# Softmax denominators: from a ones product, Ln and Exp to a transposed sum, a reciprocal and a transpose on VectorE

## The chip, the cores and the metric

The kernel runs on one core of a Trainium2 chip. The metric is the device time of a whole execution in microseconds; the number given for a kernel is the median of several executions. Beside it stands one execution taken by the hardware profiler, with every instruction of the engines TensorE (PE), VectorE (DVE), ScalarE (ACT), GpSimd (POOL) and SyncE (SP), the last of which only issues transfers here.

## The reference

Attention over 32 learned memory slots a head, followed by a gated feed-forward block. There are 8 batches of 8 heads, 576 tokens, head size 64; the feed-forward block goes from 512 to 1536 and back.

```python
a = exp(phi - max(phi, axis=2));  a = a / (sum(a, axis=2) + 1e-09)
k_m = einsum('bhsm,bhsd->bhmd', a, k);  v_m = einsum('bhsm,bhsd->bhmd', a, v)
scores = q @ k_m.T / sqrt(64)                      # per head: 576 tokens x 32 slots
attn = exp(scores - max(scores));  attn = attn / (sum(attn, axis=-1) + 1e-09)
x = attn @ v_m                                     # heads side by side: 4608 x 512
out = (silu(x @ w_gate) * (x @ w_val)) @ w_out     # 4608 x 512, float32
```

The change concerns the last division of attention: the sum over the 32 slots, for every token and head.

## The kernel before, in words

**Layout.** The scores of a batch lie with slots along the partitions: a tile `es[b, g]` of 128 partitions (four heads of 32 slots) by 2 halves of 288 tokens, for each of two groups `g` of heads. Summing over slots thus means summing over blocks of 32 partitions. `z_inv` does it with TensorE: a product with `bones`, a 128x128 matrix with four 32x32 blocks of ones on its diagonal, gives every partition the sum of its own head. ScalarE then takes Ln of it from PSUM (L427) and Exp of the negative (L429), which is the reciprocal in `lz`; both functions and the Exp of the scores are in one table. `norm` (L434) multiplies on VectorE and leaves the weights `t_A`.

**The value projection is folded.** `v_m` is multiplied into the gate and value weights first (`u_round`, tiles `t_U`), so that `gv_half` (L497) computes gate and value for 128 of 1536 features and 288 tokens by two products over `t_A`, one for each group. `gv_gate` puts a Silu on the gate (ScalarE, L513), the pending `mul` multiplies it with the value (VectorE, L520) into `t_h`. A batch has 24 such slots. `out_units` (L557) are the products of `t_h` with `w_out`: 12 for each tile of 128 tokens, then a copy of the tile from PSUM to `t_o` by VectorE (L569) or ScalarE (L567), and transfers to DRAM on SP's queue. A batch's list of out products (`out_list`) has 4 or 5 tiles, and is worked off in the batch after it: it is the filler that `take(n)` hands out wherever TensorE would wait.

**Order.** All instructions are issued in an order written out by hand (`manual_schedule`); each engine works through its own in that order. Batches 0 and 1 are done together at the start, with a code of their own. For batches 2 to 7 the loop at the end does: four out products; `u_values`, the fourth of the six parts of `t_U` (8 products, two copies at L478); `scores` for both groups, each with two Exp (L413); Exp of phi for the next batch; `z_inv` for both groups; a switch to the table with Silu (L804); `norm` for both groups. In between stand out products, 32 from the scores to the first slot. Then the 24 slots with the rest of the out products spread among them, and in their midst the key and value sums of the next batch (`kv_items`: L233 and L265 to L295), the last two parts of this batch's `t_U` (`u_item`) and the first three of the next (`u_three`). At the end of a batch comes the switch back to the table with Exp and Ln (L655).

**Other queues.** Keys, values, q and phi of later batches are loaded on POOL's queue; q is transposed by a transfer on SP's queue (`load_qT`, L120). From batch 4 on POOL also adds up Exp of phi for the next batch (`phi_sum`); it begins with a copy, `t_mark` (L213), that waits for `t_A` of group 1. PSUM has eight banks, taken from one list in turn (`bank`, `done`); `t_o` has three buffers.

Of the kernel before, what the change touches and what calls it, by code (L numbers as in the profile page):

```python
# [9 lines left out]
FP32 = mybir.dt.float32  # L10
# [4 lines left out]
def kernel(  # L15
# [19 lines left out]
    nc = tc.nc  # L35
# [8 lines left out]
    NG = 2  # L44
    NP = H // 2
    NJF = DF // 128
    HALF = S // 2
    CH = 512
    NCH = DF // CH
    sm_scale = 1.0 / math.sqrt(D)  # L50
# [347 lines left out]
    def scores(b, g):  # L398
        p = gv_banks()
        for i in range(NP):  # L400
            for r in range(2):
                nc.tensor.matmul(  # L402
                    p[r][32 * i:32 * i + 32, 0:HALF],
                    lhsT=kTs[b][64 * r:64 * r + 64, g, 32 * i:32 * i + 32],
                    rhs=qTs[b, i][64 * r:64 * r + 64, g],
                    start=True,
                    stop=True,
                    tile_position=(64 * r, 32 * i),
                )
        e = att.tile([128, 2, HALF], BF16, tag=f"E{g}", name="t_E")  # L410
        for r in range(2):
            scale = rks[b][:, g:g + 1] if b in rks else sm_scale
            nc.scalar.activation(out=e[:, r], in_=p[r][:, 0:HALF], func=AF.Exp, scale=scale)  # L413
        done(*p)
        es[b, g] = e
# [3 lines left out]
    def z_inv(b, g):  # L419

        p = gv_banks()
        lz = att.tile([128, 2, HALF], FP32, tag="lz", bufs=3, name="t_lz")
        for r in range(2):
            nc.tensor.matmul(  # L424
                p[r][:, 0:HALF], lhsT=bones, rhs=es[b, g][:, r], start=True, stop=True
            )
            nc.scalar.activation(out=lz[:, r], in_=p[r][:, 0:HALF], func=AF.Ln)  # L427
        done(*p)
        nc.scalar.activation(out=lz, in_=lz, func=AF.Exp, scale=-1.0)  # L429
        lzs[b, g] = lz  # L430

    def norm(b, g):
        a = att.tile([128, 2, HALF], BF16, tag=f"A{g}", name="t_A")
        nc.vector.tensor_tensor(out=a, in0=es.pop((b, g)), in1=lzs.pop((b, g)), op=ALU.mult)  # L434
        atts[b, g] = a
# [6 lines left out]
    def u_round(b, parts, evac):  # L442


        banks = []
        for which, c, halves in parts:
            w0, w1, h0, h1 = which[0], which[-1] + 1, halves[0], halves[-1] + 1
            n = (h1 - h0) * HC
            p = [bank([128, CH], FP32, f"p_u{g}") for g in range(NG)]
            for w in which:  # L450
                o = (w - w0) * n
                for i in range(NP):
                    for g in range(NG):
                        nc.tensor.matmul(  # L454
                            p[g][32 * i:32 * i + 32, o:o + n],
                            lhsT=kTs[b][64 * g:64 * g + 64, 2, 32 * i:32 * i + 32],
                            rhs=w_part(w, c, i, g, halves),
                            start=True,
                            stop=True,
                            tile_position=(64 * g, 32 * i),  # L460
                        )
            for g in range(NG):
                if (b, c, g) not in Us:
                    Us[b, c, g] = upool.tile([128, 2, 2, HC], BF16, tag=f"U{c}{g}", name="t_U")
                if len(which) == 1:
                    dst = Us[b, c, g][:, h0:h1, w0]
                else:
                    dst = Us[b, c, g][:, h0]
                src = p[g][:, 0:(w1 - w0) * n].rearrange("p (a f) -> p a f", f=HC)
                banks.append((dst, src, p[g], rSs[b][:, g:g + 1] if b in scaled else None))  # L470
        for (t, p, home, r), e in zip(banks, evac):
            if e == "a":
                if r is None:
                    nc.scalar.copy(out=t, in_=p)  # L474
                else:
                    nc.scalar.activation(out=t, in_=p, func=AF.Copy, scale=r)  # L476
            elif r is None:
                nc.vector.tensor_copy(out=t, in_=p)  # L478
            else:
                nc.vector.tensor_scalar(out=t, in0=p, scalar1=r, scalar2=None, op0=ALU.mult)  # L480
            done(home)
# [67 lines left out]
    def out_units(c, u, eng):  # L549

        mine = {}

        def unit(jf):
            def run():
                if jf == 0:
                    mine["p"] = bank([128, DM], FP32, "p_oo")
                nc.tensor.matmul(  # L557
                    mine["p"],
                    lhsT=hts[c, jf][:, 128 * u:128 * (u + 1)],
                    rhs=WO[jf],  # L560
                    start=(jf == 0),
                    stop=(jf == NJF - 1),
                )
                if jf == NJF - 1:
                    t_o = work.tile([128, DM], FP32, tag="to", name="t_o")
                    if eng == "a":
                        nc.scalar.copy(out=t_o, in_=mine["p"])  # L567
                    else:
                        nc.vector.tensor_copy(out=t_o, in_=mine["p"])  # L569
                    done(mine["p"])  # L570
                    for (r0, m, bb, jj, pp) in token_segments(2 * c * S + 128 * u, 128):
                        nc.sync.dma_start(
                            out=out_r[bb, jj, pp:pp + m, :], in_=t_o[r0:r0 + m, :]
                        )

            return run

        return [unit(jf) for jf in range(NJF)]
# [32 lines left out]
    def out_list(b):  # L611
        tiles = range(0, 4) if b % 2 == 0 else range(4, 9)
        res = []
        for n, u in enumerate(tiles):
            if b + 1 == B and u == tiles[-1]:
                res += out_units_end(b // 2, u)
            else:
                res += out_units(b // 2, u, "v" if n % 4 != 3 else "a")
        return res

    def q_items(b, evac):
# [15 lines left out]

    def u_values(b):

        u_round(b, (((1,), 1, (0, 1)),), "vv")  # L640
    def run(items):
        for x in items:
            x()
# [131 lines left out]
    def take(n):  # L775
        nonlocal backlog
        n = max(0, min(n, len(backlog)))
        part, backlog = backlog[:n], backlog[n:]
        return part

    for b in range(2, B):
        last = b + 1 == B
        exp_tables()
        if b == 2:
            load_qT(2)
            phi_exp(2)
            run(take(28))
            run(kv_items(2)[:1] + take(6) + kv_items(2)[1:] + take(14))
        run(take(4))
        u_values(b)  # L790
        for g in range(NG):
            scores(b, g)
        if b == 2:
            load_k(3)
            load_v(3)
            load_q(4)
            load_phi(4, nc.gpsimd)
        run(take(6))
        if not last:
            phi_exp(b + 1)  # L800
        z_inv(b, 0)
        run(take(1))
        z_inv(b, 1)
        nc.scalar.preload_act_table_set("silu_and_others")  # L804
        run(take(13))
        norm(b, 0)
        norm(b, 1)
        if b == 2:
            run(take(4))
            u_three(2)  # L810
        run(take(12))
        g = gv_slots(b)
        beside = 0 if last else 7
        outs = [lambda: run(take(1)) for _ in range(len(backlog) - beside)]
        streams = [(g, 0, 24), (outs, 0, 24)]
        if last:
            streams += [([u_item(b, 2)], 5, 6)]
        if b == 2:
            streams += [
                ([lambda: load_qT(3)], 12, 12),  # L820
                (kv_items(3, lambda: (u_item(2, 2)(), run(take(2)))), 10, 14),
                ([lambda: (run(take(2)), u_three(3), run(take(3)))], 17, 18),
            ]
        elif not last:
            load_qT(b + 1)
        if not last:
            if b > 2:
                phi_sum(b + 1)
            if b + 3 < B:
                load_q(b + 3)  # L830
            if b + 2 < B:
                load_k(b + 2)
                load_v(b + 2)
            if b + 3 < B:
                load_phi(b + 3, nc.gpsimd)
        if not last and b > 2:
            streams += [
                (kv_items(b + 1, lambda: (u_item(b, 2)(), run(take(2)))), 9, 14),
                ([lambda: (run(take(2)), u_three(b + 1), run(take(3)))], 17, 18),
            ]  # L840
        spread(*streams)
        flush_mul()
        backlog += out_list(b)
# [29 lines left out]
```

The softmax here doesn't subtract the row's maximum and nothing guards it: scores larger than these inputs give would overflow.

## Time and profile before

| | |
|---|---|
| median of 11 executions | 246.91 us (246.66 to 247.24) |
| the profiled execution, own time | 247.4 us |
| its span, first to last instruction | 245.5 us |
| TensorE busy | 233.7 us (95%), granted clock 0.999 |
| VectorE busy | 164.0 us (67%) |
| ScalarE busy | 165.0 us (67%) |
| GpSimd busy | 47.6 us (19%) |
| transfers | 37.00 MB, mean 151 GB/s |

Busy times are of engines that work beside each other, and do not add up to the span. In a row of the groups, the line, the engine and the operation come first, then what is written and what is read with the shape and the count; then the busy time in all, the mean length of one in ns, and the time that the engine idled ahead of them with what ended it. Matmuls run one into the next, so the mean length of one is more than the time that it takes from the queue; that is read from the distance between two starts. In the timeline a row has the start, the length, the engine, the line and the count; an idle time ahead of it stands in brackets with what ended it.

### The profile page before, as it was taken

What the parts mean: (1) busy time and instruction counts of PE and PEld (TensorE: products, weight loads), DVE (VectorE), ACT (ScalarE), POOL (GpSimd) and SP (SyncE); (2) the same over time, 40 slices, a digit from 0 to 9 for tenths busy, and PEclk for the clock granted to TensorE, in tenths of its full rate; (3) what the DMA queues carried; (4) which work ended last, traced back from release to release, by engine and by line L of the source; (5) the groups of instructions that cost most, each with busy time, mean ns of one, the idle gap of its engine ahead of it and who ended that gap; (6) DMA issues with size and microseconds to landing.
All of it is one profiled execution on the core that took longest, in us unless ns stands there. A gap on an engine that the chain in (4) does not pass through costs nothing.

```text
span 245.5 us, 6474 instructions
## 1 busy us (share of the span) xinstructions
PE 233.7 (95%) x2508; PEld 141.5 (58%) x2535; DVE 164.0 (67%) x368; ACT 165.0 (67%) x350; POOL 47.6 (19%) x77
## 2 busy tenths in 40 slices
PE   7997999999999999999999999999999999999993
PEld 2553567674445656477646655476546655567542
DVE  4257699992348688479837887489846876587320
ACT  2768789893096567957895677766995668676201
POOL 8432522000050004051305130070005000000000
PEclk9999999999999999999999999999999999999999
DMA  7999999996899986993995499389326221310144
GB/s 209 204 205 205 201 207 208 255 251 91 175 152 235 236 191 81 220 310 81 156 275 152 76 166 262 112 160 168 72 47 147 38 45 43 85 45 1 45 117 97
DMA packets 42447, 37.00 MB, mean 151 GB/s; under 512 B 15920, under 2 KB 37168, under 8 KB 42416
## 3 DMA queue, kind: packets, MB, share of 16 engines
q0 software_dynamic: 21424, 22.42, 52.9%
q1 hardware_dynamic: 20240, 13.37, 22.8%
q10 hardware_dynamic: 752, 0.79, 1.0%
q8 instruction: 20, 0.33, 0.5%
q14 instruction: 11, 0.09, 0.1%
HBM read 42.47 MB, written 9.44 MB: 211 GB/s over the span
## 4 chain that ended last, share of the span: by engine, by line
PE 76%; DMA 17%; POOL 3%; issue 2%; ACT 0%; POOLq 0%
PE p_oo L557 30%; PE p_g L497 19%; PE p_v L497 18%; DMA t_kv<-in_v_dram 14%; PE p_u L454 5%; DMA t_qT<-t_q 3%; PE p_kv L233 2%; POOL t_q L107 1%; POOL t_kv L97 1%; DMA out_dram<-t_o 1%; PE p_g L424 1%; PE p_v L424 0%; PE p_g L402 0%; POOL t_q L114 0%; POOL t_kv L101 0%
## 5 line engine op out<-in xcount | busy, mean ns | idle before, releaser
L557 PE MATMUL p_oo<-WO,t_h 128*128 128x512 bf16 x393 | 101.8, 379 | 3.0 <-issue 2.9
L513 ACT ACTIVATE t_sg<-p_g 128x288 bf16<-128x288 f32 x192 | 76.4, 414 | 33.5 <-PE p_g L497 26.7
L520 DVE TENSOR_TENSOR t_h<-t_sg,p_v 128x288 bf16<-128x288 bf16 x192 | 82.4, 452 | 17.3 <-PE p_v L497 12.6
L497 PEld LDWEIGHTS <-t_U 128*128 128x128 bf16 x768 | 73.8, 98 | 31.7 <-issue 2.5
L497 PE MATMUL p_g<-t_A,t_U 128*128 128x288 bf16 x384 | 77.7, 286 | 0.4
L497 PE MATMUL p_v<-t_A,t_U 128*128 128x288 bf16 x384 | 76.9, 286 | 0.0
L557 PEld LDWEIGHTS <-t_h 128*128 128x128 bf16 x420 | 39.5, 98 | 41.0 <-issue 5.9
L569 DVE COPY t_o<-p_oo 128x512 f32<-128x512 f32 x27 | 18.7, 691 | 31.4 <-PE p_oo L557 31.3
L478 DVE CAST t_U<-p_u 128x512 bf16<-128x512 f32 x42 | 26.7, 684 | 6.8 <-PE p_u L454 6.8
L474 ACT CAST t_U<-p_u 128x512 bf16<-128x512 f32 x30 | 15.8, 592 | 8.1 <-PE p_u L454 8.1
L567 ACT COPY t_o<-p_oo 128x512 f32<-128x512 f32 x8 | 4.7, 588 | 20.5 <-PE p_oo L557 10.6
L114 POOL DMA_DIRECT2D t_q<-in_q_dram x6 | 4.8, 800 | 62.7 <-DMA t_qT<-t_q 61.2
L454 PE MATMUL p_u<-W,t_kT 64*32 64x512 bf16 (+1 forms) x416 | 16.0, 364 | 0.1
L668 PE MATMUL p_warm<-bones 128*128 128x512 bf16 (+2 forms) x43 | 12.7, 423 | 1.7 <-DVE bones L691 1.7
L434 DVE TENSOR_TENSOR t_A<-t_E,t_lz 128x576 bf16<-128x576 bf16 x16 | 11.5, 751 | 0.3 <-ACT t_lz L429 0.2
L213 POOL COPY t_mark<-t_A 1x1 bf16<-1x1 bf16 x4 | 0.7, 182 | 55.7 <-DVE t_A L434 55.7
L429 ACT ACTIVATE t_lz<-t_lz 128x576 f32<-128x576 f32 x16 | 10.9, 682 | 0.5
L655 ACT ACT_TABLE_LOAD x7 | 9.0, 1283 | 1.4 <-PEq L857 1.3
L476 ACT ACTIVATE t_U<-p_u,t_rS 128x512 bf16<-128x512 f32 (+1 forms) x14 | 8.1, 628 | 2.1 <-PE p_u L454 2.1
L454 PEld LDWEIGHTS <-t_kT 64*32 64x32 bf16 x416 | 4.9, 89 | 8.0 <-issue 6.8
L480 DVE TENSOR_SCALAR t_U<-p_u,t_rS 128x512 bf16<-128x512 f32 (+1 forms) x14 | 8.8, 669 | 1.0 <-PE p_u L454 1.0
L668 PEld LDWEIGHTS <-bones 128*128 128x128 bf16 x43 | 4.4, 109 | 7.1 <-issue 3.0
(67 smaller groups left out, 169.5 us busy)
## 6 DMA issues: line engine op xcount, KB each, us to landing
t_kv<-in_k_dram POOLq DMA_DIRECT2D x8, 576.0 KB, 9.9
t_kv<-in_v_dram POOLq DMA_DIRECT2D x8, 576.0 KB, 14.1
out_dram<-t_o SPq DMA_DIRECT2D x23, 192.0 KB, 2.5
t_phi<-in_phi_dram POOLq DMA_DIRECT2D x6, 576.0 KB, 16.6
t_q<-in_q_dram POOLq DMA_DIRECT2D x6, 576.0 KB, 8.0
out_dram<-t_o SPq DMA_DIRECT2D x24, 128.0 KB, 2.6
WO<-in_moe_w_out_dram POOLq DMA_DIRECT2D x3, 512.0 KB, 19.2
out_dram<-t_o SPq DMA_DIRECT2D x23, 64.0 KB, 2.0
```

What stands on the lines that cost most here:

```text
L429: nc.scalar.activation(out=lz, in_=lz, func=AF.Exp, scale=-1.0)
L434: nc.vector.tensor_tensor(out=a, in0=es.pop((b, g)), in1=lzs.pop((b, g)), op=ALU.mult)
L454: nc.tensor.matmul(p[g][32 * i:32 * i + 32, o:o + n], lhsT=kTs[b][64 * g:64 * g + 64, 2, 32 * i:32 * i + 32], rhs=w_part(w, c, i, g, halve ...
L474: nc.scalar.copy(out=t, in_=p)
L478: nc.vector.tensor_copy(out=t, in_=p)
L497: nc.tensor.matmul(p[:, 0:HALF], lhsT=Us[b, c, g][:, o // 2, which, 128 * (o % 2):128 * (o % 2 + 1)], rhs=atts[b, g][:, r], start=(g == 0) ...
L513: nc.scalar.activation(out=sg, in_=gate[:, 0:HALF], func=AF.Silu)
L520: nc.vector.tensor_tensor(out=dst, in0=sg, in1=val[:, 0:HALF], op=ALU.mult)
L557: nc.tensor.matmul(mine["p"], lhsT=hts[c, jf][:, 128 * u:128 * (u + 1)], rhs=WO[jf], start=(jf == 0), stop=(jf == NJF - 1),)
L569: nc.vector.tensor_copy(out=t_o, in_=mine["p"])
L655: nc.scalar.preload_act_table_set("natural_log_exp_and_others")
L668: nc.tensor.matmul(p[:, 0:128 * a], lhsT=bones, rhs=x.to_broadcast([128, a, 128]) if a > 1 else bones, start=True, stop=True,)
```

## The change

The denominators of batches 2 to 7 are no longer computed by `z_inv`. A new function, `z_inv_v`, does it on VectorE alone. A sum with `apply_transpose` turns each 32x32 block of `es` (32 slots by 32 tokens) and adds along the slots, so that the sums of a token stand on the partition of its place in its block of 32 tokens: the 2 x 288 columns are 18 blocks, and the sums are a tile of 128x18. Then comes the reciprocal, and a 32x32 transpose that reads each reciprocal 32 times over and so hands it back to all 32 slots of its head. `norm` is as before. Batches 0 and 1 keep `z_inv`.

Along with it, in the same loop: `scores` are issued ahead of `u_values`; the two copies of `u_values` go from VectorE to ScalarE; Exp of phi and the switch to the Silu table follow at once, as ScalarE has no Ln and no second Exp; sum, reciprocal, transpose and `norm` are issued group by group, ahead of the 20 out products that were spread among them; and in every list of out products tiles 0 and 1 are copied by ScalarE and the others by VectorE, where it had been tile 3 by ScalarE and the others by VectorE.

```diff
+    NBL = HALF // 32
...
+    def z_inv_v(b, g):
+        z = att.tile([128, 2, 2 * NBL], FP32, tag="z", name="t_z")
+        nc.vector.tensor_reduce(
+            out=z[:, 0],
+            in_=es[b, g].rearrange("p r (n t) -> p (r n) t", t=32),
+            axis=mybir.AxisListType.X,
+            op=ALU.add,
+            apply_transpose=True,
+        )
+        nc.vector.reciprocal(out=z[:, 1], in_=z[:, 0])
+        lz = att.tile([128, 2, HALF], FP32, tag="lz", bufs=3, name="t_lz")
+        nc.vector.transpose(
+            out=lz.rearrange("p r (n t) -> p (r n) t", t=32),
+            in_=z[:, 1].rearrange("p (n t) -> p n t", t=1).to_broadcast([128, 2 * NBL, 32]),
+        )
+        lzs[b, g] = lz
...
-                res += out_units(b // 2, u, "v" if n % 4 != 3 else "a")
+                res += out_units(b // 2, u, "a" if n < 2 else "v")
...
-        u_round(b, (((1,), 1, (0, 1)),), "vv")
+        u_round(b, (((1,), 1, (0, 1)),), "aa")
...
         run(take(4))
-        u_values(b)
         for g in range(NG):
             scores(b, g)
+        u_values(b)
...
-        run(take(6))
         if not last:
             phi_exp(b + 1)
-        z_inv(b, 0)
-        run(take(1))
-        z_inv(b, 1)
         nc.scalar.preload_act_table_set("silu_and_others")
-        run(take(13))
-        norm(b, 0)
-        norm(b, 1)
+        for g in range(NG):
+            z_inv_v(b, g)
+            norm(b, g)
+        run(take(20))
```

## The prediction

> **What bounds the kernel now.** I read the page first (busy time, slices), then the chain of waits, then the groups by form, and last the timeline where attention of one batch meets the gate and value products of the same batch. All concern the profiled execution.
>
> ```profile
> PE 233.7 (95%) x2508; PEld 141.5 (58%) x2535; DVE 164.0 (67%) x368; ACT 165.0 (67%) x350; POOL 47.6 (19%) x77
> PE   7997999999999999999999999999999999999993
> ...
> PE 76%; DMA 17%; POOL 3%; issue 2%; ACT 0%; POOLq 0%
> ```
>
> TensorE is busy in nearly every slice at full clock, and it carries 76% of the chain; VectorE and ScalarE carry none of it. Busy time alone could mislead, so the timeline must show that its instructions follow each other without a hole. The groups the change touches or comes near:
>
> ```profile
> L424 PE MATMUL p_g<-t_E,bones 128*128 128x288 bf16 x16 | 4.6, 288 | 0.4 <-ACT t_E L413 0.2
> L427 ACT ACTIVATE t_lz<-p_g 128x288 f32<-128x288 f32 x16 | 6.6, 411 | 0.9 <-PE p_g L424 0.9
> L429 ACT ACTIVATE t_lz<-t_lz 128x576 f32<-128x576 f32 x16 | 10.9, 682 | 0.5
> L434 DVE TENSOR_TENSOR t_A<-t_E,t_lz 128x576 bf16<-128x576 bf16 x16 | 11.5, 751 | 0.3 <-ACT t_lz L429 0.2
> L265 DVE RECIPROCAL t_rS<-p_kv 128x2 f32<-128x2 f32 x6 | 1.0, 172 | 3.0 <-PE p_kv L233 3.0
> L392 DVE COPY t_qT<-p_q 128x576 bf16<-128x576 bf16 x8 | 3.3, 453 | 1.2 <-PE p_q L379 1.1
> ```
>
> The timeline of batch 4's attention (start, length, engine, line):
>
> ```profile
> 122.41 1.28 ACT L655 ACT_TABLE_LOAD   x1
> ...
> 123.77 0.41 ACT L413 ACTIVATE t_E<-p_g 128x288 bf16<-128x288 f32 x1
> 124.07 0.40 ACT L413 ACTIVATE t_E<-p_v 128x288 bf16<-128x288 f32 x1
> ...
> 125.06 0.29 PE L424 MATMUL p_g<-t_E,bones 128*128 128x288 bf16 x1
> 125.19 0.29 PE L424 MATMUL p_v<-t_E,bones 128*128 128x288 bf16 x1
> 125.31 0.38 PE L557 MATMUL p_oo<-WO,t_h 128*128 128x512 bf16 x1
> ...
> 129.39 1.42 DVE L434 TENSOR_TENSOR t_A<-t_E,t_lz 128x576 bf16<-128x576 bf16 x2
> 131.17 0.41 PE L497 MATMUL p_g<-t_A,t_U 128*128 128x288 bf16 x2
> ```
>
> The ones products start 0.12 to 0.13 us apart and the out product follows at once: the 288 ns of the group is latency, the queue time is 0.12 us each. The normalised weights t_A are ready at 130.81, 0.36 us before TensorE wants them, so nobody waits here. The last view is the one place after the start where a transfer holds TensorE, in batch 2, at the key and value sums of batch 3:
>
> ```profile
> 84.32 0.80 PE L233 MATMUL p_kv<-t_kv,t_ephi 64*32 64x128 bf16 x72 [0.40 <-DMA t_kv<-in_v_dram]
> ```
>
> **The change, part by part.**
>
> *Ones products off TensorE.* Four per batch. From 125.06 to 125.31 two take 0.25 us, the next two (125.53 to 125.77 in the same timeline) 0.24: 0.49 us a batch, all on the path. Six batches make 2.94 us.
>
> *Batch 2's share goes into a transfer.* Values of batch 3 are issued at 68.64 and land 15.6 us later, at 84.28. They stand on POOL behind a load of q that waits for the transposing transfer of batch 2, issued at 60.03 once its own q had landed (issued 40.10, 19.8 us). None of that chain hangs on a TensorE instruction that gets earlier. TensorE comes 0.49 us sooner and waits 0.89 instead of 0.40. So five batches count: 5 x 0.49 = **2.45 us**. I looked for the next such place: values of batch 4 are issued at 96.22, land at the latest 12.8 us later (109.0) and are wanted at 110.66, or 110.17 now; those of batch 5 (117.17 + 12.4 = 129.6) are wanted at 137.45, about 1 us sooner now. Both hold.
>
> *The new chain on VectorE.* For each group: transposed sum over 128x576, reciprocal of 128x18 (18 blocks of 32 tokens), transpose to 128x576, then the unchanged product. No row shows the first three.
> - Sum and transpose: the nearest row is the product of the same 576 columns, 751 ns (576 cycles at 0.96 GHz are 600, the rest is fixed). Below, the copy of 128x576 bf16 at 453 ns, two columns a cycle; above, two cycles a column, 150 + 1200 = 1350 ns. I take 0.75 each.
> - Reciprocal: row L265, 172 ns for two columns; 16 more at a cycle each give 0.19. The casts of 64x64 and 64x128 from PSUM (223 and 289 ns) put the fixed part at 157, which leaves 15 ns for two columns, some 7 cycles each. The Trainium skill, "VectorE: DVE Perf Modes", First, the fixed hardware budget, says that a reciprocal is an iterative divide with a repeat count of 8: 18 x 8 / 0.96 GHz = 0.15 plus 0.15 fixed, an estimate of 0.30. No row settles it; I take the dear 0.30. By the cheap one the chain is 0.2 us shorter and the forecast the same.
> - Each dependent step starts about 0.03 us after the one ahead (recip 61.97 + 0.17, next 62.17).
>
> A group: 0.75 + 0.30 + 0.75 + 0.75 + 0.12 = 2.67 us; two: 5.34. It starts when group 0's second Exp ends, 124.47. Exp starts right behind the table load (122.41 + 1.28 = 123.69), so scores issued ahead of the u product bring nothing. The chain ends at 124.5 + 5.3 = 129.8. TensorE gets to L497 at 131.17 - 0.49 = 130.68, its group 1 product 0.12 later. Margin about **0.9 us**; the stall begins when the chain is longer than 6.3 us (130.80 - 124.47) and eats the gain from 6.8 us on. The cover is the 32 out products (216 ns each, 6.9 us). Batches 3, 5, 6 and 7 have the same stage (7.99 or 8.00 us from the u product to L497, as batch 4 from 123.17 to 131.17); batch 2's is 9.74 us long (67.38 to 77.12) and has 2 us more of cover.
>
> A rule that speaks against: the Trainium skill, "Vector Engine (DVE) Microarchitecture Reference", 5.2 Measured stream behaviour on trn2, says that a port keeps its rate only where consecutive elements come in runs of two or more adjacent words; a source hopping at every element took 1.73 ns a column and not 1.05. The transpose reads each reciprocal 32 times over, step 0, not a run. The page measures hops, not a repeated word, so I keep the row. If the rule holds, the transpose is 150 + 576 x 1.73 = 1.15 us (an estimate), the chain 5.34 + 2 x 0.40 = 6.1: most of the margin is gone, but the sum is the same.
>
> *What waits behind the chain.* VectorE's in-order queue: the sum waits for E; behind the chain stand the out copy of tile 2 (done 130.88 on TensorE, as late as the 131.37 of before less 0.49) and the first gate product (131.9). Both come after 129.8. POOL's mark (L213) waits for group 1's product, now some 1 us earlier; its sums then take 4 us and are wanted at 136.8.
>
> *ScalarE.* Gone: four Ln and two Exp, 4 x 0.41 + 2 x 0.68 = 3.0 us. New: two u casts (0.59 each) and the out copies of tiles 0 and 1. From 125.09: casts to 126.1, exp of phi 1.18 to 127.3, table 1.28 to 128.6, copies (tiles finish on TensorE near 125.7 and 128.3) to 129.8. The first Silu comes at 131.1. Cost nothing, 1.3 us of cover. If u casts are late, banks of p_u stay held until 126.1; their next use is beyond L497.
>
> *Out copies.* Tile 3 of every list goes from ScalarE (0.59) to VectorE (0.69) inside the gate stage. VectorE there is busy 15.35 of 17.79 us (105.45 to 123.24) and now 16.0; at 139.42 it already lags by two casts (1.28 us) without holding TensorE, through eight banks. Nothing, with 0 to 0.2 us in three batches as bound. On SP the out transfers keep their order: tile 0's leaves 2 to 3 us later, but load_qT stands behind tile 2's, which moves with TensorE. No transfer is added or removed.
>
> *Sum:* 247.4 us for this execution (245.5 span, 1.9 around it) less 2.45 = 244.95. The median shown is 246.91, 0.5 lower; the forecast in medians is 246.91 - 2.45 = **244.5**.
>
> **The rivals.**
>
> *The chain comes late by a little:* one of the two passes, say the fp32 transpose, needs two cycles a column (0.60 more each). Chain 5.34 + 1.20 = 6.54, stall 0.24 in five batches, gain 5 x 0.25 = 1.25: 245.7; with 6.4 to 6.7 for the chain 245.0 to 246.5. For it: a margin of 0.9 over three instructions that no row shows, and twice the bytes in fp32. Against: the fp32 rows named below run at full rate.
>
> *VectorE's 32 by 32 passes need two cycles a column, slower than before.* One mechanism: the array that turns the block does not fill while it empties. Then sum and transpose cost 1.35 each, the chain 5.34 + 4 x 0.60 = 7.74, TensorE waits 1.44 at L497 in batches 3 to 7, and 5 x (1.44 - 0.49) = 4.75 us are lost: 251.7. It decides from a chain of 6.8 us on, that is 0.36 us more on each of the four passes. For it: no row shows such a pass. Against: VectorE reads an fp32 operand in L434 and writes fp32 in the out copies (128x512 in 691 ns) at a column a cycle.
>
> *The products go and nothing comes of it:* TensorE held elsewhere, in other batches by transfers as in batch 2, or by banks behind the moved copies. The margins above (1.1 us at the least) speak against. 246.9.
>
> **How the numbers follow.** Likeliest case 0.65 (243.9 to 244.9); little late 0.12; no change 0.05; slower 0.18. About 0.2% is what a measurement of this kernel can tell from no change, 0.5 us; so faster 0.77, same 0.05, slower 0.18. The range goes from 243.7 (batch 2's half microsecond kept as well, and a little) to 246.8, which takes in the late chain and most of the no-change case and leaves the slow passes out.
>
> **What would show it.** Right: L424 left with 4 + 4 products; the span about 2.4 us shorter; the wait at the sums of batch 3 grown from 0.40 to about 0.9; from E of group 0 to the end of group 1's product 5 to 5.5 us; L497 behind the out products without a hole, the stage from its first score or u product to L497 down from 8.00 to about 7.51. Wrong: a TensorE wait at L497 for t_A; a sum or transpose over 1.0 us; waits of TensorE for VectorE at the moved copies; batch 3 to 7 not each 0.49 shorter.

## The result, and the profile after

| | before | after |
|---|---|---|
| median | 246.98 us (31 executions) | 244.4 us (8 executions, 244.02 to 244.59) |
| ratio to before, 95% interval | | 0.989 (0.9878 to 0.9902) |
| profiled execution, own time | 247.4 us | 244.37 us |
| its span | 245.5 us | 242.6 us |
| VectorE, ScalarE busy | 164.0, 165.0 us | 172.0, 160.5 us |

The kernel is faster by 2.6 us in medians, 2.4 to 3.0 us by the interval of the ratio, and by 2.9 us in the spans of the two profiles. Line numbers move: L497 is now L517, L557 is L577, L434 is L454, L233 is L234.

Busy time by engine, and the chain by engine, of the changed kernel:

```profile
PE 231.0 (95%) x2484; PEld 139.2 (57%) x2511; DVE 172.0 (71%) x384; ACT 160.5 (66%) x334; POOL 47.5 (20%) x77
...
PE 86%; DMA 7%; POOL 2%; issue 2%; DVE 1%; ACT 0%; DVEq 0%; POOLq 0%
```

VectorE took on 8 us and is still no more than 1% of the chain. TensorE lost 2.7 us of busy time and stays the bound. Transfers fell from 17% of the chain to 7%: the values of batch 3, whose landing had ended a wait of TensorE, are no longer part of it. The groups of the new chain, by form (the third number is the mean in ns):

```profile
L437 DVE TRANSPOSE_TENSOR_REDUCE t_z<-t_E 128x18 f32<-128x576 bf16 x12 | 9.3, 775 | 6.4 <-ACT t_E L414 6.4
L444 DVE RECIPROCAL t_z<-t_z 128x18 f32<-128x18 f32 x12 | 3.2, 266 | 0.4
L446 DVE STREAM_TRANSPOSE t_lz<-t_z 128x576 f32<-128x576 f32 x12 | 9.3, 779 | 0.4
L454 DVE TENSOR_TENSOR t_A<-t_E,t_lz 128x576 bf16<-128x576 bf16 x16 | 12.1, 757 | 0.8 <-ACT t_lz L430 0.2
```

The idle time ahead of the sum, 6.4 us, is VectorE waiting for E: it comes early, not late. The same stage of batch 4 in the timeline:

```profile
121.29 1.28 ACT L675 ACT_TABLE_LOAD   x1
...
122.11 0.29 PE L403 MATMUL p_g<-t_qT,t_kT 64*32 64x288 bf16 x1
...
122.89 0.41 ACT L414 ACTIVATE t_E<-p_v 128x288 bf16<-128x288 f32 x1
...
123.33 0.78 DVE L437 TRANSPOSE_TENSOR_REDUCE t_z<-t_E 128x18 f32<-128x576 bf16 x1 [1.20 <-ACT t_E L414]
...
124.14 0.27 DVE L444 RECIPROCAL t_z<-t_z 128x18 f32<-128x18 f32 x1
124.44 0.78 DVE L446 STREAM_TRANSPOSE t_lz<-t_z 128x576 f32<-128x576 f32 x1
...
127.85 0.76 DVE L454 TENSOR_TENSOR t_A<-t_E,t_lz 128x576 bf16<-128x576 bf16 x1
...
129.62 0.41 PE L517 MATMUL p_g<-t_A,t_U 128*128 128x288 bf16 x2
```

From the end of E (123.30) to the end of group 1's product (127.85 + 0.76 = 128.61) are 5.3 us. TensorE comes to L517 at 129.62: about a microsecond to spare, and no idle time stands in brackets ahead of it. From the first score (122.11) to L517 the stage takes 7.51 us, where it had taken 8.00.

Where the 2.9 us of this pair of executions came from is read from the starts of the four out products that open each batch, before and after:

| end of batch | before | after | gained in this batch |
|---|---|---|---|
| 2 | 96.50 | 95.93 | 0.57 |
| 3 | 122.22 | 121.16 | 0.49 |
| 4 | 150.52 | 148.97 | 0.49 |
| 5 | 176.26 | 174.33 | 0.38 |
| 6 | 204.56 | 202.15 | 0.48 |
| 7 (start of the last tile's products) | 238.89 | 235.98 | 0.50 |

(The traced execution of the kernel before is 0.4 us slower than its median, so the table speaks for this pair alone.) Batches 3 to 7 gave 2.34 us. Batch 2, which the prediction had put at nothing, gave 0.57, out of a gain and a loss:

```profile
83.40 0.80 PE L234 MATMUL p_kv<-t_kv,t_ephi 64*32 64x128 bf16 x72
...
86.56 0.68 DVE L589 COPY t_o<-p_oo 128x512 f32<-128x512 f32 x1
86.70 0.41 PE L517 MATMUL p_g<-t_A,t_U 128*128 128x288 bf16 x2
...
87.30 0.41 PE L517 MATMUL p_v<-t_A,t_U 128*128 128x288 bf16 x2 [0.19 <-DVE t_o L589]
```

The sums of batch 3 start at 83.40, with no wait for the values, where they had started at 84.32 after a wait of 0.40: 0.92 us gained. Then the copy of tile 3, now on VectorE, holds TensorE up. The bracket counts 0.19 us from the end of the products ahead; from start to start the two rows of L517 around the copy lie 0.60 us apart instead of 0.24. By the next u product 0.35 us are lost: it comes 7.05 us after the sums (90.45), where it had come 6.70 us after them (91.02).

### The profile page after: what moved, and what is told of

Read it like the earlier page. It is cut to its first block, busy times and chain, and to the rows that moved or that the text cites. A ratio compares the mean times of both kernels' runs of the same rounds, so it can differ in the third digit from the quotient of the medians.

```text
span 242.6 us, 6431 instructions
## 1 busy us (share of the span) xinstructions
PE 231.0 (95%) x2484; PEld 139.2 (57%) x2511; DVE 172.0 (71%) x384; ACT 160.5 (66%) x334; POOL 47.5 (20%) x77
## 4 chain that ended last, share of the span: by engine, by line
PE 86%; DMA 7%; POOL 2%; issue 2%; DVE 1%; ACT 0%; DVEq 0%; POOLq 0%
PE p_oo L577 36%; PE p_g L517 20%; PE p_v L517 20%; DMA t_kv<-in_v_dram 7%; PE p_u L474 5%; PE p_kv L234 2%; PE p_oo L609 1%; POOL t_q L108 1%; PE p_g L403 1%; POOL t_kv L98 1%; DVE t_U L498 0%; POOL t_kv L102 0%; PE p_mT L322 0%; DVE t_o L589 0%; PE p_T L294 0%
## 5 line engine op out<-in xcount | busy, mean ns | idle before, releaser
L577 PE MATMUL p_oo<-WO,t_h 128*128 128x512 bf16 x393 | 100.0, 379 | 2.9 <-issue 2.7
L540 DVE TENSOR_TENSOR t_h<-t_sg,p_v 128x288 bf16<-128x288 bf16 x192 | 82.1, 451 | 15.6 <-PE p_v L517 12.5
L517 PEld LDWEIGHTS <-t_U 128*128 128x128 bf16 x768 | 73.8, 98 | 32.0 <-issue 2.7
L517 PE MATMUL p_g<-t_A,t_U 128*128 128x288 bf16 x384 | 77.7, 286 | 0.4
L517 PE MATMUL p_v<-t_A,t_U 128*128 128x288 bf16 x384 | 76.9, 286 | 0.2 <-DVE t_o L589 0.2
L577 PEld LDWEIGHTS <-t_h 128*128 128x128 bf16 x420 | 39.6, 98 | 43.2 <-issue 6.4
L494 ACT CAST t_U<-p_u 128x512 bf16<-128x512 f32 x42 | 22.5, 604 | 7.9 <-PE p_u L474 7.9
L589 DVE COPY t_o<-p_oo 128x512 f32<-128x512 f32 x19 | 13.1, 688 | 17.4 <-PE p_oo L577 13.0
L498 DVE CAST t_U<-p_u 128x512 bf16<-128x512 f32 x30 | 19.0, 683 | 1.5 <-PE p_u L474 1.5
L437 DVE TRANSPOSE_TENSOR_REDUCE t_z<-t_E 128x18 f32<-128x576 bf16 x12 | 9.3, 775 | 6.4 <-ACT t_E L414 6.4
L587 ACT COPY t_o<-p_oo 128x512 f32<-128x512 f32 x16 | 8.9, 587 | 7.4 <-PE p_oo L577 7.3
L454 DVE TENSOR_TENSOR t_A<-t_E,t_lz 128x576 bf16<-128x576 bf16 x16 | 12.1, 757 | 0.8 <-ACT t_lz L430 0.2
L414 ACT ACTIVATE t_E<-p_g 128x288 bf16<-128x288 f32 x12 | 5.0, 414 | 7.1 <-PE p_v L403 7.0
L446 DVE STREAM_TRANSPOSE t_lz<-t_z 128x576 f32<-128x576 f32 x12 | 9.3, 779 | 0.4
## 6 DMA issues: line engine op xcount, KB each, us to landing
t_phi<-in_phi_dram POOLq DMA_DIRECT2D x6, 576.0 KB, 15.6
```

The costliest lines, as they stand in the source:

```text
L437: nc.vector.tensor_reduce(out=z[:, 0], in_=es[b, g].rearrange("p r (n t) -> p (r n) t", t=32), axis=mybir.AxisListType.X, op=ALU.add, appl ...
L446: nc.vector.transpose(out=lz.rearrange("p r (n t) -> p (r n) t", t=32), in_=z[:, 1].rearrange("p (n t) -> p n t", t=1).to_broadcast([128, ...
L517: nc.tensor.matmul(p[:, 0:HALF], lhsT=Us[b, c, g][:, o // 2, which, 128 * (o % 2):128 * (o % 2 + 1)], rhs=atts[b, g][:, r], start=(g == 0) ...
L540: nc.vector.tensor_tensor(out=dst, in0=sg, in1=val[:, 0:HALF], op=ALU.mult)
L577: nc.tensor.matmul(mine["p"], lhsT=hts[c, jf][:, 128 * u:128 * (u + 1)], rhs=WO[jf], start=(jf == 0), stop=(jf == NJF - 1),)
```

## The experiments

**Is the gain the queue time of the ones products?** The products come back, unread:

```diff
+        kept = [es[b, g] for g in range(NG)]
         for g in range(NG):
             z_inv_v(b, g)
             norm(b, g)
-        run(take(20))
+        run(take(6))
+        ones_unread(kept[0])
+        run(take(1))
+        ones_unread(kept[1])
+        run(take(13))
```

`ones_unread` issues the two products of `bones` with one group's `es`, and nobody reads their sums.

> The changed kernel with the four ones products of each batch from 2 on put back on TensorE, their sums not read by anyone. Theory, the gain is TensorE's queue time of the products: 0.49 us in each of six batches comes back, 244.4 + 2.9 = 247.3, at the kernel before or 0.4 above it (the moved copy of tile 3 in batch 2 stays). Rival, the gain came from what ScalarE no longer does and from the new order: it stays at 244.4.

Measured: 247.33 us, ratio to before 1.0017 (1.0008 to 1.0027). A batch begins with the switch to the Exp table; here are the starts of batches 3 and 4, of the changed kernel and then of this one:

```profile
96.07 1.28 ACT L675 ACT_TABLE_LOAD   x1
121.29 1.28 ACT L675 ACT_TABLE_LOAD   x1
```

```profile
96.56 1.28 ACT L681 ACT_TABLE_LOAD   x1
122.27 1.28 ACT L681 ACT_TABLE_LOAD   x1
```

From one switch to the next, batches 2 to 6 take 41.61, 25.71, 28.31, 25.85 and 28.30 us, where the changed kernel takes 41.11, 25.22, 27.82, 25.36 and 27.81: 0.49 to 0.50 us more in every one. The gain is the TensorE time of the products, all of it; the rest of the change, with what ScalarE no longer does, is worth nothing by itself, and by the interval costs 0.2 to 0.7 us.

**How much room has the VectorE chain?** The transpose is done more often, with the same result. For the three kernels, k is 1 for group 0 alone, 1 for both, 2 for both:

```diff
-        nc.vector.transpose(
-            out=lz.rearrange(...), in_=z[:, 1].rearrange(...).to_broadcast(...))
+        for _ in range(1 + k):
+            nc.vector.transpose(
+                out=lz.rearrange(...), in_=z[:, 1].rearrange(...).to_broadcast(...))
```

> The changed kernel with the transpose of group 0 done twice, same result: the VectorE chain is 0.8 us longer in each batch. In the trace of the changed kernel the chain of batch 4 ends at 128.61 and TensorE comes to group 1's product at about 129.74: margin 1.1 us. Theory, the chain is hidden up to its margin: 244.4, within 0.3. Rival, VectorE already holds TensorE up in part: 246 or more.

> As before it, with the transposes of both groups done twice: chain longer by 1.6 us. Theory: 1.6 - 1.1 = 0.5 us of wait at the first gate product in batches 3 to 7, none in batch 2: 244.4 + 2.5 = 246.9. Rival, other cover (banks, order) hides it: 244.4.

> Both transposes done three times: chain longer by 3.2 us. Theory, beyond the margin each microsecond of chain costs one in each of five batches, and batch 2 begins to feel it (its margin is some 2.5 to 3): 244.4 + 5 x 2.1 + 0.5 = 255.4. Rival, other work fills the wait: under 251.

Measured: 244.47 us (ratio 0.9905, 0.9888 to 0.9921), 247.61 (1.0029, 1.001 to 1.0048) and 256.79 (1.0415, 1.0387 to 1.0442). The waits of TensorE, from the list of waits of the second and of the third kernel (in all, times, longest):

```profile
PE p_g L518 <- DVE t_A L455: 2.1, 5, 0.5
```

```profile
PE p_g L518 <- DVE t_A L455: 10.6, 5, 2.5
```

The first kernel has no such wait and comes out as expected. The five waits are those of batches 3 to 7. The other two are slower than expected, 247.61 for 246.9 and 256.79 for 255.4. Against the changed kernel, batches 3 to 6 of the second grow by 0.48 to 0.62 us for 1.6 us of chain, so the room is about 1.05 us; from the second to the third they grow by 1.62 to 1.76 for another 1.6. Below the room a longer chain is free; above it each microsecond costs about one in each of five batches. Batch 2 has more room, but the third kernel passes it: the batch grows from 41.11 to 42.06 us, as a cast of t_U stands on VectorE behind the chain and TensorE waits for it:

```profile
77.76 0.30 PE L518 MATMUL p_g<-t_A,t_U 128*128 128x288 bf16 x1 [0.78 <-DVE t_U L499]
```

This is the mechanism of the prediction's slower case, shown at its price, with repeated transposes in the place of slow ones.

**Do the moves matter?** First the new functions alone, in the place of the old, nothing moved:

```diff
         run(take(6))
         if not last:
             phi_exp(b + 1)
-        z_inv(b, 0)
+        z_inv_v(b, 0)
         run(take(1))
-        z_inv(b, 1)
+        z_inv_v(b, 1)
```

> The kernel before with z_inv_v in the place of z_inv for batches 2 to 7 and nothing moved: u copies on VectorE ahead of the sums, tiles 0 and 1 copied by VectorE between the transposes and the products. Theory, the end of the VectorE chain decides: casts to 124.93 in the old timeline, two sums to transposes 3.7 us to 128.7, two out copies to 130.0, two products to 131.4, where TensorE comes to group 1 at 130.8; a wait of about 0.6 us in five batches against 0.49 saved, so 247 to 247.5, no gain. Rival, only the products on TensorE count and VectorE has room: 244.4 as with the whole change.

Measured: 245.13 us, ratio 0.9929 (0.991 to 0.9949): the price of staying put was overrated. Batch 4's stage of this kernel:

```profile
122.72 1.29 DVE L498 CAST t_U<-p_u 128x512 bf16<-128x512 f32 x2 [0.35 <-PE p_u L474]
...
127.50 1.25 DVE L589 COPY t_o<-p_oo 128x512 f32<-128x512 f32 x2
128.67 1.41 DVE L454 TENSOR_TENSOR t_A<-t_E,t_lz 128x576 bf16<-128x576 bf16 x2
129.75 0.67 PE L517 MATMUL p_g<-t_A,t_U 128*128 128x288 bf16 x2
```

The casts and two out copies now stand in the chain, and the products end at 130.08. Two products of L517 usually take 0.41 us here and took 0.67: 0.26 us of wait for group 1, not 0.6. Batches 3 to 6 are 0.19 to 0.32 us longer than in the changed kernel; batch 2, where tile 3 is still copied by ScalarE, is 0.36 us shorter (40.75 for 41.11). Instructions of VectorE that do not read each other's result overlap by some 0.1 us (two out copies in 1.25, two products in 1.41, where one takes 0.69 and 0.76), which the expectation had left out. So the swap alone already pays. The moves bring a further 0.7 us in the medians (245.13 and 244.4), about what a wait of 0.26 us in each of five batches makes, less the 0.36 of batch 2. Which of the moves takes the wait away was not tried.

Then the moves alone, with `z_inv` as before on TensorE and ScalarE:

```diff
-        u_values(b)
         for g in range(NG):
             scores(b, g)
+        u_values(b)
...
-        u_round(b, (((1,), 1, (0, 1)),), "vv")
+        u_round(b, (((1,), 1, (0, 1)),), "aa")
...
-                res += out_units(b // 2, u, "v" if n % 4 != 3 else "a")
+                res += out_units(b // 2, u, "a" if n < 2 else "v")
```

> The kernel before, with z_inv as it was on TensorE and ScalarE, and of the change only the moves: scores ahead of the u product, its two copies on ScalarE, tiles 0 and 1 copied by ScalarE. Theory: the moves bring nothing by themselves, 246.9 within 0.5; ScalarE's queue gets longer by 2.4 us and the first Silu comes some 0.8 us later than before, which the eight banks take up. Rival, the moves are part of the gain: 246.0 or less; or ScalarE holds TensorE up: 248 or more.

Measured: 253.37 us, ratio 1.0254 (1.0222 to 1.0285), so the expectation failed. Batches 3 to 5 take 25.72, 28.30 and 25.71 us, as before the change (25.77, 28.25, 25.80); the loss is in batch 2 (43.11 against 41.72), where TensorE waits for a PSUM bank until ScalarE has copied the tile in it, and above all in batch 6 (34.57 against 28.24), where one transfer comes late:

```profile
75.46 0.41 PE L454 MATMUL p_u<-W,t_kT 64*32 64x512 bf16 x7 [1.12 <-ACT t_o L567]
...
164.21 7.44 SPq L120 DMA_TRANSPOSE t_qT<-t_q  x1
...
181.84 0.42 PE L402 MATMUL p_g<-t_qT,t_kT 64*32 64x288 bf16 x1 [3.42 <-DMA t_qT<-t_q]
```

On SP's queue the transposing transfer stands behind the out transfers of tiles 0 to 2. Tiles 0 and 1 are now copied by ScalarE, which still has Ln, Exp and the u casts ahead of them, so the queue moves late: the transfer is issued at 164.21, just behind POOL's load of keys (164.15). In the kernel before it was issued at 161.28, two microseconds ahead of that load (163.30). It lands 17.6 us after its issue and not 9.4. The order of issues and the landings are in the traces; that the loads ahead of it are what slows it was not tried. In the full change ScalarE is rid of Ln and Exp: in batch 4 it copies tiles 0 and 1 6.0 us after the table load that opens the batch (127.24), and here 8.6 us after it. The transfer that comes late here is issued at 159.24 there, 1.5 us ahead of the load of keys (160.69). The moves need the swap.

**Tile 3's copy.** Tiles 0, 1 and 3 on ScalarE:

```diff
-                res += out_units(b // 2, u, "a" if n < 2 else "v")
+                res += out_units(b // 2, u, "v" if n in (2, 4) else "a")
```

> The changed kernel with the out copy of tile 3 of every list back on ScalarE (tiles 0, 1, 3 there, 2 and 4 on VectorE). Theory, the moved copy costs 0.35 us once, in batch 2, where it stands on VectorE behind two casts and TensorE waits for a bank: 244.0 to 244.1, and no wait of TensorE for t_o. Rival, the 0.35 us lost there is the transfer's or chance: 244.4 and the wait of batch 2 elsewhere.

Measured: 244.27 us, ratio to before 0.9884 (0.9868 to 0.9901). Its interval overlaps that of the change, so the medians show no gain. The trace does show the 0.35 us. From the sums of batch 3 to the next u product before the change are 6.70 us (84.32 to 91.02), in the changed kernel 7.05, here 6.70 again (83.50 to 90.20), and no wait for t_o is left. In this execution TensorE waited 0.32 us for the values instead.

**When do the values of batch 3 land?** The kernel before once more, for its trace:

> The kernel before once more, for its trace: when the values of batch 3 land. Theory, the landing (84.28 in the first trace, 15.6 us after the issue) varies from execution to execution by a microsecond or more: it lands at another time here. Rival, it is tied to this kernel's order of out copies: 84.3 again, with a wait of TensorE of about 0.4 us.

It took 248.11 us in its one profiled execution, and the values landed 16.0 us after their issue (15.6 in the first trace):

```profile
84.97 0.80 PE L233 MATMUL p_kv<-t_kv,t_ephi 64*32 64x128 bf16 x72 [0.98 <-DMA t_kv<-in_v_dram]
```

The issue was later too (68.9 instead of 68.64), and TensorE waited 0.98 us. So the wait itself moves by 0.6 us from one execution to another. Both traces of this kernel have a late landing, while the changed kernel has 14.0, its variants above 13.9 to 15.1, the swap alone 14.4, the moves alone 11.9. But both are executions slower than the median, by 0.4 and 1.1 us, so they may not be the usual case. The next run moves only the out copies that lie in this window:

```diff
-                res += out_units(b // 2, u, "v" if n % 4 != 3 else "a")
+                res += out_units(b // 2, u, "a" if n % 4 == 3 or (b == 1 and n < 2) else "v")
```

> The kernel before, with two copies moved: tiles 0 and 1 of batch 1's list (worked off in batch 2) are copied by ScalarE, behind its table load near 74.3, and not by VectorE at 70.4 and 73.0. Their transfers to DRAM so leave later, and not while the values of batch 3 are on their way. Theory, these transfers are what makes the values land late in the kernel before (15.6 and 16.0 us after their issue, 11.9 to 15.1 in all kernels in which the copies are later): landing within 14.5 us. Rival, it is something else: 15.5 or more again.

One execution of 247.97 us: 15.0 us, between the two cases. The keys issued just ahead of the values landed after 10.7 us, where both traces of the kernel before have 12.8 and the changed kernel 9.4. TensorE did not wait for the values, but 0.36 us for the bank of a moved copy. The out transfers are not the whole answer, if they are a part of it; with one execution each and a spread of half a microsecond, what sets the landing stays open.

**A faster version?** Tile 3 on ScalarE, and the scaling of the value sums too:

```diff
-            scaled_copy(bv[:, g], p[g][:, D:2 * D], rSs[b][:, g:g + 1])
+            nc.scalar.activation(
+                out=bv[:, g], in_=p[g][:, D:2 * D], func=AF.Copy, scale=rSs[b][:, g:g + 1])
```

> A try at a faster version: the changed kernel with tile 3 copied by ScalarE and with the scaling of the value sums (t_bv, two instructions of 276 ns) on ScalarE instead of VectorE, beside the scaling of the key sums. TensorE waits for t_bv five times, 0.9 to 1.1 us in all, as the banks of the sums come free. Theory, that wait goes: 243.3 to 243.6. Rival, the u casts of ScalarE come later by as much and take its place: 244.3 as before.

Measured: 244.18 us, ratio to before 0.9886 (0.9866 to 0.9907). The five waits for t_bv are gone from the list of waits, and the time is not measurably below that of the change: removing them brought nothing that can be told from 244.4.

## Why the prediction was right

The forecast was 244.5 us, the median is 244.4; the likeliest case is the one that happened, and its mechanism held. That the number is so close is in part luck: of the two terms of batch 2 that the sum had put at nothing, one was a gain and the other a loss.

- **Ones products, 0.49 us a batch.** Right, and shown by putting them back: 0.49 to 0.50 in each batch, 247.33 in all.
- **The chain on VectorE.** Predicted 5.34 us, measured 5.3. Sum and transpose were taken at 0.75 and took 775 and 779 ns; the reciprocal was taken dear at 0.30 and took 266 ns, between the two estimates (0.19 and 0.30) and nearer to the iterative divide. The rule that the prediction names against the transpose, and doubted, does not carry over to one word read 32 times: 779 ns, where it would have made 1.15 us.
- **The room.** Predicted 0.9 us, a stall from a chain of 6.3 us on and no gain left from 6.8 us on. Measured 1.05 us of room (a chain of 6.35), and the kernel with 1.6 us more, a chain of 6.9, at 1.0029 of before. Both slower cases needed sums or transposes of 1.35 us; they take 0.78.
- **Batch 2's share lost to the transfer.** Wrong. The step said that the values land at 84.28 because nothing in their chain hangs on an instruction that gets earlier. The issue was indeed the same (68.66), but in the traced execution the landing came 14.0 us after it and not 15.6, and TensorE did not wait at all: 0.92 us gained up to there, where the step had nothing. One profiled landing was taken for a fixed time.
- **Out copies at nothing, 0 to 0.2 us in three batches as bound.** Wrong in batch 2: 0.35 us, as the copy of tile 3 stands right behind two casts on VectorE. In batches 4 and 6 the same copy cost nothing: from the sums to the next u product they take 7.38 and 7.37 us, before the change 7.37 both. The step had read the slack of eight banks from batch 4 alone.
- **The sum.** These two misses leave batch 2 with 0.57 us, so the span fell by 2.9 and not by 2.45. The medians fell by 2.58. The two traced executions of the kernel before are slower than its median of 246.98 by 0.4 and 1.1 us, about as much as TensorE waits in them for the values (0.40 and 0.98). If a usual execution does not wait there, the change gains the ones products of all six batches less the copy of tile 3: 6 x 0.49 - 0.35 = 2.59. The kernel with the products put back, 0.46 us above the kernel before in the medians, agrees. This is worked out and not shown, as no execution of the kernel before without the wait was traced.
- **Waits behind the chain.** Right: the out copy of tile 2 (129.82) and VectorE's first product with a gate (130.84) wait for TensorE and not for the chain, and POOL's mark comes earlier (at 128.68, where it had come at 130.87).

## What to carry to other kernels

Work taken from an engine that is busy without a hole is worth its queue time, the distance of two starts and not its mean duration, if what replaces it ends before that engine gets there: find the two times in the timeline, and the difference is the budget. Beyond the budget each microsecond cost about one in every round of this loop; a step done twice shows where it ends. Moves that help beside a swap may do harm without it, as they lengthen another queue, so try both parts alone. Do not take the landing of one transfer in one trace for a constant, and compare a traced execution with the median before you explain a few tenths of a microsecond by what its trace shows.

## What the runs showed of the hardware

The transposed sum and the 32 by 32 transpose, the latter in fp32 and from a source that repeats one word, take about as long as a plain VectorE instruction: 775 and 779 ns for 576 columns against 757 for a product of the same width. So VectorE can sum over blocks of 32 partitions at the price of such a product.

In the wait of 3.42 us in batch 6 of the kernel with the moves alone, the granted clock of TensorE fell to half and stayed there after it (a row has a stretch of time and its length, the busy time of PE, PEld, DVE, ACT and POOL, the granted clock, and the DMA share and GB/s):

```profile
178.40:181.80 3.40, 0.02 (x1) 0.00 (x0) 0.00 (x0) 0.41 (x1) 0.00 (x0) 0.85 1.13 136
181.80:186.80 5.00, 4.63 (x35) 1.98 (x37) 0.00 (x0) 4.21 (x10) 0.00 (x0) 0.50 0.03 5
```

In steps of 0.4 us the clock is at half from 180.8, 2.4 us after the last product before the wait, to 187.6, 5.8 us after the first one behind it. At half the clock 5.8 us do the work of 2.9; with the wait that makes 6.3 us, by which batch 6 grew. So in this execution the late transfer cost nearly twice its wait. It is the slowest of six; the fastest, with 251.78 us, has a mean granted clock of 0.998 where this one has 0.986.

The Trainium skill, "TensorE: Matmul & The Clock Gate", Part 1: The HAM clock gate, says that an idle window of about 3.4 us halves the clock until a busy one of about as much has passed. The halving agrees; the times here, 2.4 and 5.8 us, are not those of the page. Nor does every wait of that length halve the clock: those of up to 2.5 us in the kernel with the longest chain left its mean granted clock at 1.0.
